# Left-over rows in places of their own, and sums of w_in formed from the operands in SBUF

## The chip, the cores and the metric

One core of one Trainium2 chip runs the kernel. The metric is device time in microseconds (us). Engines are named as in the profile: PE (matmul), PEld (its weight load), DVE (VectorE), ACT (ScalarE), POOL (GpSimd) and SP, which issues most DMAs.

## What is computed

Linear attention for 8 batches of 8 heads (576 rows, 64 columns a head), and then a gated MLP on its 4608 rows of 512 columns:

```python
q_s = softmax(q, axis=-1); k_s = softmax(k, axis=2)
kv = einsum('bhsd,bhse->bhde', k_s, v)
x  = einsum('bhsd,bhde->bhse', q_s, kv)      # heads side by side: (4608, 512)
h = x @ w_in                                  # w_in (512, 2048)
out = (h * cos(h)) @ w_out                    # w_out (2048, 512)
```

The inputs are drawn as 64-bit numbers and arrive as pairs of 32-bit words.

## The kernel before

**Tiles.** A batch gives 512 "main" rows of x and 64 left-over rows; the left-over rows of all eight batches form a ninth block of 512, collected in the HBM tensor `x_left`. A pair of heads is called p (0 to 3), a block b, a 128-wide slice of the MLP's inner dimension f (0 to 15). Each f32 operand of the MLP is held as a high and a low part, and a product takes three matmuls (hi·hi, hi·lo, lo·hi). For blocks 0 to 4 a unit (b, f) is twelve matmuls into `h` (L842), the gate on ACT and DVE (`gated`: L867, L871, L877, L882), the split into `ghi` and `glo` (L898, L902), and twelve matmuls into `acc` (L926; for the first six units eight, L919). Blocks 5 to 8 go in two pairs by `block` (L1170), with seven products in place of eight; these need sums and differences of quarters of w_in.

**Weights.** `load_w` brings a 512 KB tile of w_in (`raw_i`) or w_out (`raw_o`), and `convert` turns the 64-bit words into f32: `bias` and `bits` on ACT (L397, L402), `shift` and `sign` on DVE (L408, L419) into the place `wc`, then `hi` (L428) and `lo` (L432). For w_in, `keep` then stores the f32 rows in the HBM tensor `w_rows` (L442, SP). Later `sums(n)`, n = 0 to 7, loads two such rows back (`rows`, L997), forms sums on DVE (L1002 to L1005), splits them (L1009, L1013) and stores them in `w_sums` (L1020). `own` stores the halves of w_in themselves in `w_own` (L1023). `block` loads both through POOL (L1144).

**Attention at the start.** For block 0 and each p: column maxima of k on DVE (L536 to L545) and POOL (L551), difference and exp (L558, L564), the product kv (L602), its scaled copy `kvw` (L622); q's softmax (L649 to L668), its transpose on PE (L694, L698) and the copy `qf` (L710); then `x_mm` (L715) in two halves, the high part `x_hi` (L729), and for block 0 a second product less the high part (L715, L720) for the low part (L738). `x_hi` also copies the left-over 64 columns (L732) to `xl`, and `put` stores them (L754). For blocks below QD = 2 both `qf` and `xl` take places of the same ring `row`, which has three. From block 2 on, q is transposed through HBM into the place `qb` (L767).

**Order.** Every step is entered in a `Plan` with an engine, a duration, reads, writes and a due time; a list scheduler with these durations decides one order for all engines, and each engine then works in that order. A load has a step on SP and one on a modelled bus. The program has eight semaphores for SP's DMAs, so each issue waits until the one eight issues before has landed. An instruction that waits holds up all that stand behind it on its engine.

Of the kernel before, what the change touches and what calls it, by code (L numbers as in the profile page):

```python
# [11 lines left out]
F32 = mybir.dt.float32  # L12
# [13 lines left out]
CFG = dict(  # L26
    FH=8,
    XF=8,
    PELO=1,
    early=1,  # L30
    F2=6,
    FN=8,
    QD=2,
    warm=14,
# [8 lines left out]
    att0=dict(k=(-11.28, 5.44), kv=(18.78, -0.31), q=(5.83, 11.45), qt=(12.05, 4.95), x=(9.45, -8.71)),  # L43
    att1=(5.98, 6.97),
    std=5,
    slow=1.3,
    spans={2: (15.0, 28.0), 3: (29.0, 42.0), 4: (43.0, 56.0), 5: (52.0, 66.0), 6: (62.0, 77.0)},
    phi=0.906,
# [157 lines left out]
def linear_attention_then_cos_gated_mlp(  # L206
# [18 lines left out]
    nc = tc.nc  # L225
    B, H, S, D = q.shape
    DM = H * D
    DFF = w_in.shape[1]
    P = 128
    NP = H // 2  # L230
    CM = S // P
    NM = CM * P
    NL = S - NM
    NC = CM + 1
    KC = DM // P
    NF = DFF // P
# [12 lines left out]
    dr = ctx.enter_context(tc.tile_pool(name="dr", bufs=1, space=bass.MemoryType.DRAM))  # L249
# [38 lines left out]
    q_rows = dr.tile([2, S, P], F32, name="q_rows")  # L288
    part = dr.tile([2, NJ, P, DM], F32, name="part")
    x_main = dr.tile([B, KC, P, TB], F32, name="x_main")  # L290
    w_rows = dr.tile([NF, P, DM], F32, name="w_rows")
    w_sums = dr.tile([NF // 2, P, 4, 2, 2 * P], F32, name="w_sums")
    w_own = dr.tile([NF, P, 2, DM], F32, name="w_own")

    plan = Plan()
    plan.add("POOL", 9.0, None)
    T = {}
# [6 lines left out]
    def ring(tag):  # L304

        i = nth.get(tag, 0)
        nth[tag] = i + 1
        return (tag, i % BUFS[tag])
# [6 lines left out]
    def sbt(shape, dt, tag, name):  # L315

        pool = small if tag[0] in SMALL else sb
        return pool.tile(shape, dt, tag=tag if isinstance(tag, str) else f"{tag[0]}{tag[1]}", name=name, bufs=1)
# [63 lines left out]
    def convert(w, f):  # L382

        fs = [f] if f < FN else [base(f), base(f) + 1]
        n = len(fs)
        R = [("w", w, x) for x in fs]
        wait = w == "o" and f < F2
        C = room(f) if wait else ring("wc")

        def low():  # L390
            return T["raw", w, f][0][:, :, :, 0]

        def high():
            return T["raw", w, f][0][:, :, :, 1]

        def bias():
            nc.scalar.activation(  # L397
                high().bitcast(F32), high().bitcast(F32), AF.Identity, scale=2.0**-112
            )

        def bits():
            nc.scalar.activation(  # L402
                low().bitcast(I32), low(), AF.Identity, bias=0.4996, scale=0.875 * 2.0**-29
            )

        def shift():
            x, y = low().bitcast(I32), high().bitcast(I32)
            nc.vector.scalar_tensor_tensor(  # L408
                x, y, 3, x, op0=ALU.logical_shift_left, op1=ALU.bitwise_or
            )  # L410

        def sign():
            if wait:
                if ("room", f // 4) not in T:
                    T["room", f // 4] = sbt([P, 4, DM], F32, f"wo{room(f)[1]}", f"room_{f // 4}")
                c = T["wc", w, f] = T["room", f // 4][:, f % 4 : f % 4 + 1]
            else:
                c = T["wc", w, f] = sbt([P, 2, DM], F32, C, f"wc_{w}{f}")[:, 0:n]
            nc.vector.scalar_tensor_tensor(  # L419
                c.bitcast(I32), high().bitcast(I32), -(2**31), low().bitcast(I32),  # L420
                op0=ALU.bitwise_and, op1=ALU.bitwise_or,
            )

        def hi():
            t = T["wp", w, f] = sbt([P, n, 2, DM], F32R, spot(w, f), f"w_{w}{f}")
            for i, x in enumerate(fs):
                T["w", w, x] = t[:, i]
            nc.scalar.copy(t[:, :, 0], T["wc", w, f])  # L428

        def lo():  # L430
            t = T["wp", w, f]
            nc.vector.tensor_sub(t[:, :, 1], T["wc", w, f], t[:, :, 0].bitcast(F32))  # L432

        act, dve = (0.66, 0.69) if n == 1 else (1.1, 1.22)
        plan.add("ACT", act, bias, writes=R)
        plan.add("ACT", act, bits, writes=R)
        plan.add("DVE", dve, shift, writes=R)
        plan.add("DVE", dve, sign, reads=R, writes=[C])

        def keep():  # L440
            for i, x in enumerate(fs):
                nc.sync.dma_start(w_rows[x], T["wc", w, f][:, i])  # L442

        def split():
            plan.add("ACT", act - 0.04, hi, reads=[C], writes=R)
            plan.add("DVE", dve, lo, reads=[C], writes=R)

        if wait:
            splits[f] = split
        else:  # L450
            split()
        if w == "i":
            plan.load(0.73 * n, keep, reads=[C], writes=[("rows", x) for x in fs], parts=n)


    def load_k(b, p0, np_, tag, due, seq=()):
# [220 lines left out]
    def x_steps(b, p, place, kvw, tq, tx, due_q, due_x):  # L677
# [46 lines left out]
        def x_hi(i):  # L724
            if i == 0:
                T["x", b, p] = sbt([P, 2, TB], F32R, slot, f"x_{b}_{p}")
            cs = cols[i]
            o = T["xp", b, p, i, False]
            nc.scalar.copy(T["x", b, p][:, 0, cs], o[:, 0 : cs.stop - cs.start])  # L729
            if i == 1:  # L730
                t = T["xs", b, p] = sbt([P, NL], F32, xs, f"xl_{b}_{p}")
                nc.scalar.copy(t, o[:, TB - HALF : HALF])  # L732

        def x_lo(i):
# [40 lines left out]

        qr = [(place, 0), (place, 1)]
        cold = 2.0 if b == 0 and p < CFG["cold"] else 1.0
        qf, xs = ring("row"), ring("row")
        if blocks:
            qd, qb = ring("qd"), ring("qb")  # L780
            plan.load(1.1, q_out, reads=qr, writes=[qd], parts=2, due=due_q)
            plan.load(2.3, q_in, reads=[qd], writes=[qb], parts=4)
            plan.add("DVE", 0.75, q_blocks, reads=[qb], writes=[qf])
        else:
            if (b, p) in CFG["fill_q"]:
                fill(o1, 24, ("fill", "q", b, p), f"qt1_{b}_{p}", o1, due_q)
            plan.add(
                "PE", (0.44 if odd else 0.55) * cold, q_tr, reads=qr, writes=[o1] if odd else [o1, o2],
                due=due_q,
            )  # L790
            if not odd:
                plan.add("ACT", 0.23, q_side, reads=[o2], writes=[ring("ql")])
            plan.add("ACT", 0.82, q_f32, reads=[o1, o2], writes=[qf])
# [195 lines left out]
    def sums(n):  # L989

        f = 2 * n
# [2 lines left out]

        def rows():
            t = T["sum", n] = sbt([P, 2, DM], F32, s, f"sum_{n}")
            nc.sync.dma_start(t, w_rows[f : f + 2].rearrange("f p d -> p f d"))  # L997

        def adds():
            t = T["sum", n].rearrange("p f (k d) -> p (f k) d", k=2)  # L1000
# [21 lines left out]
        def own(x, k):  # L1022
            nc.sync.dma_start(w_own[x, :, :, k * 2 * P :], T["w", "i", x].bitcast(F32)[:, :, k * 2 * P :])  # L1023

        plan.load(0.73 * 2, rows, reads=[("rows", f), ("rows", f + 1)], writes=[s], due=due)
        plan.add("DVE", 1.8, adds, writes=[s])
        plan.add("ACT", 1.1, hi, reads=[s], writes=quarters(hs))
        plan.add("DVE", 1.22, lo, reads=quarters(hs), writes=[s])
# [2 lines left out]
        for k in range(2):  # L1031
            plan.load(
                1.46 - 0.73 * k, lambda k=k: own(f + k, k), reads=[("w", "i", f + k)], writes=[("own", f + k)],
                due=when((CFG["std"] - 2.5 + 0.18 * n) * NF),
            )

# [245 lines left out]
    def when(pos):  # L1282
        return T0 + U * pos
# [153 lines left out]
```

## Time and profile before

| | us |
|---|---|
| median of 3 runs (879.75 to 880.63) | 879.84 |
| the profiled execution's own time | 879.14 |
| its span in the trace | 877.30 |
| PE busy in the span | 855.6 |
| DVE, ACT, POOL busy | 596.9, 523.3, 77.9 |
| moved by DMA | 138.69 MB |

Times in rows are counted from the span's start. The profiled execution took 1.84 us more than its span, and the median of the runs lies 0.70 us above the profiled execution. A row of a timeline gives start, duration, engine, line, operation, output and inputs, and in brackets how long the engine had been idle and what ended that.

### The profile page before, as it was taken

The page shows a single profiled execution, that of the slowest core. Times are in us where ns is not written, and L with a number is a line of the kernel's source. Part 1 is how long each engine was busy: PE and PEld are TensorE (multiplying, and loading weights), DVE is VectorE, ACT ScalarE, POOL GpSimd, SP SyncE. Part 2 cuts the span into 40 slices and gives each one's busy share as a digit, 9 for nine tenths or more (in the row PEclk, how much of TensorE's full clock was granted, in tenths as well). Part 3 has the DMA queues.
Part 4 walks back from the last instruction along what each step waited for, and adds up shares of the span by engine and source line. Part 5 has one row for each costly group of instructions (what it writes and reads, how often), then busy time and mean ns, then how long its engine had stood idle before and what let it go on. Part 6 is the DMA issues. An engine that isn't in the chain of part 4 may idle for free.

```text
span 877.3 us, 12066 instructions
## 1 busy us (share of the span) xinstructions
PE 855.6 (98%) x4192; PEld 689.8 (79%) x4192; DVE 596.9 (68%) x961; ACT 523.3 (60%) x878; POOL 77.9 (9%) x149
## 2 busy tenths in 40 slices
PE   6889999999999999999999999999999999999998
PEld 4666688888887887888888877888888888888876
DVE  7698989996865855765885778675447937444542
ACT  3788898756555646664766646665446635444541
POOL 2100100010010010001000002111010201111000
PEclk8789999999999999999999999999999999999999
DMA  8995499924643531633797637966243726243212
GB/s 207 330 285 188 134 348 288 267 60 130 171 113 101 124 67 44 173 80 100 187 300 205 229 110 185 238 155 183 80 122 108 237 75 192 84 143 97 61 38 83
DMA packets 202556, 138.69 MB, mean 158 GB/s; under 512 B 113920, under 2 KB 174848, under 8 KB 202496
## 3 DMA queue, kind: packets, MB, share of 16 engines
q1 hardware_dynamic: 189184, 108.56, 43.9%
q0 software_dynamic: 13312, 29.36, 12.0%
q8 instruction: 33, 0.54, 0.3%
q14 instruction: 27, 0.22, 0.1%
HBM read 94.11 MB, written 43.78 MB: 157 GB/s over the span
## 4 chain that ended last, share of the span: by engine, by line
PE 93%; DMA 2%; SPq 2%; ACT 2%; DVE 1%; issue 0%; ACTq 0%
PE acc L926 42%; PE h L842 25%; PE z L1170 10%; PE a L1170 7%; PE x_False L715 4%; PE acc L919 2%; PE kv L602 2%; DMA x_left<-xl 1%; DMA raw_i<-in_moe_w_in_dram 1%; SPq L493 0%; PE qt L694 0%; SPq L489 0%; DVE kt L871 0%; PE x_True L715 0%; SPq L474 0%
## 5 line engine op out<-in xcount | busy, mean ns | idle before, releaser
L842 PE MATMUL h<-x,w_i 128*128 128x512 f32 x960 | 236.2, 397 | 0.2 <-DVE kt L882 0.2
L842 PEld LDWEIGHTS h<-x,w_i 128*128 128x128 f32 x960 | 180.8, 190 | 40.6 <-DVE kt L882 0.8
L926 PE MATMUL acc<-w_o,ghi 128*128 128x512 f32 x592 | 187.8, 398 | 0.0
L926 PEld LDWEIGHTS acc<-w_o,ghi 128*128 128x128 f32 x592 | 110.3, 188 | 24.0
L926 PE MATMUL acc<-w_o,glo 128*128 128x512 f32 x296 | 115.5, 390 | 0.0
L1170 PE MATMUL z<-xs,s 128*128 128x512 f32 x384 | 97.8, 392 | 0.5 <-DVE kt L882 0.5
L867 ACT ACTIVATE kt<-h 128x512 int32<-128x512 f32 x80 | 47.6, 597 | 67.8 <-PE h L842 66.0
L1170 PEld LDWEIGHTS z<-xs,s 128*128 128x128 f32 x384 | 71.9, 188 | 16.0 <-DVE kt L882 0.9
L871 DVE SCALAR_TENSOR_TENSOR kt<-kt,h 128x512 f32<-128x512 int32 x80 | 54.5, 682 | 40.3 <-ACT kt L867 40.1
L898 ACT CAST ghi<-kt 128x512 fp32r<-128x512 f32 x74 | 45.7, 618 | 49.9 <-PE acc L926 47.5
L1170 PE MATMUL a<-xs,s 128*128 128x512 f32 x288 | 73.9, 392 | 0.4 <-DVE kt L882 0.4
L902 DVE TENSOR_TENSOR glo<-kt,ghi 128x512 fp32r<-128x512 f32 x74 | 51.1, 690 | 31.1 <-ACT ghi L898 30.8
L926 PEld LDWEIGHTS acc<-w_o,glo 128*128 128x128 f32 x296 | 55.5, 188 | 12.0
L1170 PEld LDWEIGHTS a<-xs,s 128*128 128x128 f32 x288 | 53.9, 188 | 12.2 <-DVE kt L882 0.5
L882 DVE TENSOR_TENSOR kt<-kt,h 128x512 f32<-128x512 f32 x74 | 50.3, 681 | 17.0 <-ACT kt L877 16.3
L877 ACT ACTIVATE kt<-kt 128x512 f32<-128x512 f32 x80 | 50.4, 632 | 18.9 <-DVE kt L871 18.5
L715 PE MATMUL x_False<-qf,kvw 128*128 128x288 f32 x128 | 40.2, 430 | 2.8 <-ACT kvw L622 2.8
L1144 POOL DMA_DIRECT2D s<-w_sums x32 | 20.2, 631 | 176.0 <-PE a L1170 129.3
L1191 DVE TENSOR_TENSOR c<-a,c 128x512 f32<-128x512 f32 x32 | 22.1, 691 | 19.4 <-PE a L1170 18.3
L551 POOL PARTITION_ALL_REDUCE m<-m x32 | 26.2, 843 | 98.6 <-DVE m L545 98.4
L602 PEld LDWEIGHTS kv<-v_sb,k 128*64 128x64 f32 x600 | 21.1, 146 | 15.9 <-issue 8.6
L715 PEld LDWEIGHTS x_False<-qf,kvw 128*128 128x128 f32 x128 | 25.4, 202 | 10.4 <-ACT kvw L622 3.0
(617 smaller groups left out, 1411.5 us busy)
## 6 DMA issues: line engine op xcount, KB each, us to landing
s<-w_sums POOLq DMA_DIRECT2D x32, 512.0 KB, 4.0
q<-in_q_dram SPq DMA_DIRECT2D x32, 256.0 KB, 4.2
raw_i<-in_moe_w_in_dram SPq DMA_DIRECT2D x16, 512.0 KB, 5.7
raw_o<-in_moe_w_out_dram SPq DMA_DIRECT2D x16, 512.0 KB, 6.0
out_dram<-o SPq DMA_DIRECT2D x32, 256.0 KB, 2.8
s<-w_own POOLq DMA_DIRECT2D x16, 512.0 KB, 4.3
v_sb<-in_v_dram SPq DMA_DIRECT2D x30, 256.0 KB, 3.8
k<-in_k_dram SPq DMA_DIRECT2D x14, 512.0 KB, 4.6
```

What stands on the lines that cost most here:

```text
L551: nc.gpsimd.partition_all_reduce(T["m", b, p0][:, hs].rearrange("p h d -> p (h d)"), T["m1", b, p0][:, hs].rearrange("p h d -> p (h d)"), ...
L602: nc.tensor.matmul(x[h * D : (h + 1) * D, odd : odd + vt.shape[1]], t[:, h, c, :], vt, start=(c == CM), stop=(c == CM - 1),)
L715: nc.tensor.matmul(t[:, 0:HALF], T["kv", b, p], T["qf", b, p][:, cs], start=True, stop=not again)
L842: nc.tensor.matmul(o, a, x, start=(c == 0 and n == 0), stop=(c == KC - 1 and n == 2))
L867: nc.scalar.activation(t.bitcast(I32), src(), AF.Identity, bias=0.25, scale=1.0 / TWO_PI)
L871: nc.vector.scalar_tensor_tensor(t, t.bitcast(I32), -TWO_PI, src(), op0=ALU.mult, op1=ALU.add)
L877: nc.scalar.activation(t, t, AF.Sin, bias=0.5 * math.pi)
L882: nc.vector.tensor_mul(o, t, src())
L898: nc.scalar.copy(t, T["g", u])
L902: nc.vector.tensor_sub(t, T["g", u], T["gh", u].bitcast(F32))
L926: nc.tensor.matmul(T["acc", j], a[:, js], w, start=(first and n == 0), stop=(last and n == 2))
L1170: nc.tensor.matmul(o, a, x, start=(first and c == 0 and m == 0), stop=(c == 1 and m == 2), skip_group_check=not first,)
```

## The change

- Blocks 0 and 1: `xl` no longer takes a place of the ring `row`; the eight pieces (two blocks, four p) have places of their own in one tile that lies in `qb`, and the first load into `qb` (block 2, p = 0) waits until all eight are stored. The ring `row` then serves `qf` alone for these blocks.
- `w_rows`, its 16 stores (256 KB each) and its 8 loads (512 KB each) go. `rows` now adds the high and low parts of w_in on DVE: two additions of 128x512 for n below 4, one of 128x1024 for n from 4 on.
- `own`'s 16 stores may not stand before 205 us of the plan's own time.

```diff
+    own=205.0,
-    w_rows = dr.tile([NF, P, DM], F32, name="w_rows")
-        def keep():
-            for i, x in enumerate(fs):
-                nc.sync.dma_start(w_rows[x], T["wc", w, f][:, i])
-        if w == "i":
-            plan.load(0.73 * n, keep, reads=[C], writes=[("rows", x) for x in fs], parts=n)
...
-                t = T["xs", b, p] = sbt([P, NL], F32, xs, f"xl_{b}_{p}")
+                t = T["xs", b, p] = left_rows()
...
-        qf, xs = ring("row"), ring("row")
+        qf, xs = ring("row"), ring("row") if blocks else ("x_left", CFG["QD"] * p + b)
+        def left_rows():
+            if blocks:
+                return sbt([P, NL], F32, xs, f"xl_{b}_{p}")
+            if "x_left" not in T:
+                T["x_left"] = sbt([P, CFG["QD"] * NP, NL], F32, ("qb", 0), "x_left_rows")
+            return T["x_left"][:, xs[1]]
-            plan.load(2.3, q_in, reads=[qd], writes=[qb], parts=4)
+            old = [("x_left", i) for i in range(CFG["QD"] * NP)] if b == CFG["QD"] and p == 0 else []
+            plan.load(2.3, q_in, reads=[qd], writes=[qb, *old], parts=4)
...
-            nc.sync.dma_start(t, w_rows[f : f + 2].rearrange("f p d -> p f d"))
+            if f < FN:
+                for i in range(2):
+                    w = T["w", "i", f + i].bitcast(F32)
+                    nc.vector.tensor_add(t[:, i], w[:, 0], w[:, 1])
+            else:
+                w = T["wp", "i", f].bitcast(F32)
+                nc.vector.tensor_add(t, w[:, :, 0], w[:, :, 1])
...
-        plan.load(0.73 * 2, rows, reads=[("rows", f), ("rows", f + 1)], writes=[s], due=due)
+        plan.add(
+            "DVE", 1.38 if f < FN else 1.22, rows, reads=[("w", "i", f), ("w", "i", f + 1)],
+            writes=[s], due=due,
+        )
...
                 1.46 - 0.73 * k, lambda k=k: own(f + k, k), reads=[("w", "i", f + k)], writes=[("own", f + k)],
+                after=CFG["own"],
```

With other steps in the plan, the scheduler gives another order from the first microseconds on. Three places follow. In rows of the changed kernel the lines of attention stand six lower than in the kernel before (L558 there is L564 here) and those of the gate two higher.

Place one, ACT, first exps of block 0; `raw_i` and `raw_o` are weight tiles that have just been loaded. Before:

```order
L402 ACTIVATE raw_i_220<-raw_i_220 128x512
L564 ACTIVATE k_0_171<-k_0_171 128x640
L710 COPY qf_0_293<-qt_0_0_283 128x512
L710 COPY qf_0_293<-qt_0_0_288 128x64
L564 ACTIVATE k_1_183<-k_1_183 128x640
L704 COPY ql_0_305<-qt_0_0_288 128x64
L397 ACTIVATE raw_i_271<-raw_i_271 128x512
L656 ACTIVATE q_1_226<-q_1_226 128x1152
L622 ACTIVATE kvw_0_173<-kv_0_256,r_0_325 64x64 x2
```

The changed kernel, the same stretch, and after it the copies kvw_0 and kvw_1:

```order
L402 ACTIVATE raw_i_219<-raw_i_219 128x512
L397 ACTIVATE raw_i_249<-raw_i_249 128x512
L558 ACTIVATE k_0_170<-k_0_170 128x640
L402 ACTIVATE raw_i_249<-raw_i_249 128x512
L558 ACTIVATE k_1_176<-k_1_176 128x640
L650 ACTIVATE q_1_225<-q_1_225 128x1152
...
L616 ACTIVATE kvw_0_172<-kv_0_275,r_0_303 64x64 x2
L397 ACTIVATE raw_i_270<-raw_i_270 128x512
L704 COPY qf_1_346<-qt_0_1_331 128x512
L704 COPY qf_1_346<-ql_0_327 128x64
L397 ACTIVATE raw_o_288<-raw_o_288 128x512
L616 ACTIVATE kvw_1_174<-kv_1_306,r_1_349 64x64 x2
```

The first step of the second w_in tile now stands ahead of the exps of k_0 and k_1, and that of the first w_out tile ahead of kvw_1. On SP the second tile's load stands one place earlier, ahead of the second load of v, and the first load of k for block 1 stands behind one more w_in tile, one more w_out tile and one more load of v.

Place two, DVE, last maxima of block 0 and first of block 1 (mt_0 and mt_2 read the k of block 1 that a DMA has brought; r_3 is the reciprocal for kvw_3). Before:

```order
L536 TENSOR_TENSOR mt_0_399<-k_0_323 128x512
L558 TENSOR_TENSOR k_3_185<-k_3_185,m_3_387 128x640
L541 TENSOR_TENSOR m_1_0_432<-mt_0_399 128x256
L610 TENSOR_SCALAR r_2_436<-kv_2_401 128x1
...
L610 TENSOR_SCALAR r_3_473<-kv_3_448 128x1
...
L536 TENSOR_TENSOR mt_2_543<-k_2_483 128x512
```

The changed kernel:

```order
L530 TENSOR_TENSOR mt_0_433<-k_0_344 128x512
L552 TENSOR_TENSOR k_3_184<-k_3_184,m_3_418 128x640
L535 TENSOR_TENSOR m_1_0_449<-mt_0_433 128x256
L604 TENSOR_SCALAR r_2_455<-kv_2_407 128x1
...
L530 TENSOR_TENSOR mt_2_491<-k_2_404 128x512
L604 TENSOR_SCALAR r_3_498<-kv_3_470 128x1
```

r_3 has moved behind mt_2; mt_0 stands ahead of the subtraction for k_3 in both.

Place three, ACT and DVE, the first gates (kt_632 and kt_625 are unit 0; g is its gated value; q_0 is here the q of block 1). ACT before:

```order
L564 ACTIVATE k_2_483<-k_2_483 128x1280
L867 ACTIVATE kt_650<-h_616 128x512
L877 ACT_TABLE_LOAD
L877 ACTIVATE kt_632<-kt_632 128x512
L622 ACTIVATE kvw_1_446<-kv_1_562,r_1_586 64x64 x2
```

and in the changed kernel:

```order
L558 ACTIVATE k_2_404<-k_2_404 128x1280
L869 ACTIVATE kt_625<-h_502 128x512
L616 ACTIVATE kvw_1_507<-kv_1_559,r_1_582 64x64 x2
L397 ACTIVATE raw_o_354<-raw_o_354 128x512
L879 ACT_TABLE_LOAD
L879 ACTIVATE kt_625<-kt_625 128x512
```

DVE before:

```order
L649 TENSOR_REDUCE qm_0_669<-q_0_596 128x18
L882 TENSOR_TENSOR g_676<-kt_632,h_493 128x512
L652 TENSOR_TENSOR q_0_596<-q_0_596,qm_0_669 128x1152
```

and in the changed kernel:

```order
L643 TENSOR_REDUCE qm_0_649<-q_0_590 128x18
L604 TENSOR_SCALAR r_2_665<-kv_2_638 128x1
L607 RECIPROCAL r_2_665<-r_2_665 128x1
L646 TENSOR_TENSOR q_0_590<-q_0_590,qm_0_649 128x1152
L873 SCALAR_TENSOR_TENSOR kt_668<-kt_668,h_609 128x512
L884 TENSOR_TENSOR g_681<-kt_625,h_502 128x512
```

The copy kvw_1 of block 1 has moved ahead of the table load; the gate of unit 0 has moved behind q's subtraction and the second unit's first DVE step.

## Rows read from the trace of the kernel before

**Rows 1.** The page: busy time of PE, and in 40 slices of the span the clock granted to PE, in tenths.

```profile
PE 855.6 (98%) x4192; PEld 689.8 (79%) x4192; DVE 596.9 (68%) x961; ACT 523.3 (60%) x878; POOL 77.9 (9%) x149
...
PEclk8789999999999999999999999999999999999999
```

**Rows 2.** Busy time by stretch: the stretch and its length, then for PE, PEld, DVE, ACT, POOL busy us and instructions, granted clock (1.00 is 2.4 GHz, 0.50 is 1.2 GHz), DMA's busy share, GB/s.

```profile
14.90:20.40 5.50, 5.02 (x49) 3.99 (x49) 5.47 (x11) 1.44 (x4) 1.37 (x2) 0.50 0.83 238
35.20:38.30 3.10, 3.04 (x9) 2.46 (x10) 1.63 (x3) 2.67 (x10) 1.01 (x2) 0.52 1.04 350
38.30:48.95 10.65, 10.63 (x80) 8.07 (x79) 8.23 (x15) 10.26 (x26) 1.74 (x4) 1.00 1.06 322
...
53.00:59.00 6.00, 5.95 (x32) 4.88 (x33) 5.93 (x13) 5.36 (x8) 0.00 (x0) 0.53 0.96 316
60.00:200.00 140.00, 140.00 (x647) 106.91 (x646) 125.37 (x187) 113.44 (x185) 9.19 (x20) 1.00 0.71 212
500.00:520.00 20.00, 19.75 (x103) 15.83 (x102) 14.42 (x26) 11.03 (x19) 0.00 (x0) 1.00 0.40 129
520.00:540.00 20.00, 19.14 (x99) 14.96 (x98) 17.43 (x30) 12.84 (x25) 3.80 (x6) 1.00 0.84 214
```

**Rows 3.** Two of PE's waits from 10 to 56 us: us in total, times, the longest.

```profile
PE kv L602 <- ACT k L564: 2.3, 2, 1.2
PE qt L694 <- ACT qf L710: 2.2, 2, 1.8
```

**Rows 4.** Timeline of PE.

```profile
14.92 1.35 PE L602 MATMUL kv<-v_sb,k 128*64 128x66 f32 x20 [3.64 <-DMA v_sb<-in_v_dram]
...
23.18 2.29 PE L715 MATMUL x_False<-qf,kvw 128*128 128x288 f32 x4 [2.79 <-ACT kvw L622]
...
26.47 1.86 PE L715 MATMUL x_False<-qf,kvw 128*128 128x288 f32 x4
...
36.17 2.12 PE L715 MATMUL x_False<-qf,kvw 128*128 128x288 f32 x4
...
39.45 1.13 PE L715 MATMUL x_False<-qf,kvw 128*128 128x288 f32 x4
...
41.71 0.65 PE L715 MATMUL x_True<-qf,kvw 128*128 128x288 f32 x2
...
42.42 1.39 PE L602 MATMUL kv<-v_sb,k 128*64 128x66 f32 x40
...
50.10 0.80 PE L602 MATMUL kv<-v_sb,k 128*64 128x66 f32 x20 [1.17 <-ACT k L564]
53.05 1.35 PE L602 MATMUL kv<-v_sb,k 128*64 128x66 f32 x20 [2.15 <-ACT kvw L622]
54.34 5.00 PE L842 MATMUL h<-x,w_i 128*128 128x512 f32 x12
...
59.18 3.59 PE L919 MATMUL acc<-room,g 128*128 128x512 f32 x8
```

**Rows 5.** The chain that ended last, in order of time: start, us, what.

```profile
62.78 2.75 PE h L842 x12
...
72.94 0.97 PE x_False L715 x4
```

**Rows 6.** Timeline of ACT.

```profile
12.34 0.72 ACT L564 ACTIVATE k<-k 128x640 f32<-128x640 f32 x1
...
24.47 0.62 ACT L622 ACTIVATE kvw<-kv,r 64x64 f32<-64x64 f32 x2
...
25.54 0.67 ACT L397 ACTIVATE raw_i<-raw_i 128x512 f32<-128x512 f32 x1
...
34.63 0.70 ACT L710 COPY qf<-qt 128x512 f32<-128x512 f32 x2 [2.00 <-DMA x_left<-xl]
...
50.56 1.28 ACT L877 ACT_TABLE_LOAD   x1
...
69.43 0.70 ACT L710 COPY qf<-qt 128x512 f32<-128x512 f32 x2 [0.48 <-PE qt L694]
```

**Rows 7.** Timeline of DVE. L610 is the first of two like steps of a reciprocal r.

```profile
30.43 0.69 DVE L536 TENSOR_TENSOR mt<-k 128x512 f32<-128x512 f32 x1 [3.10 <-DMA k<-in_k_dram]
31.04 0.82 DVE L558 TENSOR_TENSOR k<-k,m 128x640 f32<-128x640 f32 x1
...
41.91 0.69 DVE L536 TENSOR_TENSOR mt<-k 128x512 f32<-128x512 f32 x1 [2.07 <-DMA k<-in_k_dram]
...
52.14 1.34 DVE L649 TENSOR_REDUCE qm<-q 128x18 f32<-128x1152 f32 x1
53.41 0.68 DVE L882 TENSOR_TENSOR g<-kt,h 128x512 f32<-128x512 f32 x1
54.00 1.35 DVE L652 TENSOR_TENSOR q<-q,qm 128x1152 f32<-128x1152 f32 x1
...
55.87 0.22 DVE L610 TENSOR_SCALAR r<-kv 128x1 f32<-128x1 f32 x1
```

**Rows 8.** Issues on SP's queue: start, us to issue.

```profile
13.65 0.62 SPq L512 DMA_DIRECT2D v_sb<-in_v_dram  x1
...
21.69 0.59 SPq L374 DMA_DIRECT2D raw_o<-in_moe_w_out_dram  x1
...
43.36 0.64 SPq L512 DMA_DIRECT2D v_sb<-in_v_dram  x1
...
45.67 1.54 SPq L493 DMA_DIRECT2D q<-in_q_dram  x1
...
47.93 1.03 SPq L493 DMA_DIRECT2D q<-in_q_dram  x1
```

**Rows 9.** DMA issues in the windows of the second w_in tile (16.28 us) and of the first w_out tile (21.69 us): KB, us from issue to landing.

```profile
raw_i<-in_moe_w_in_dram SPq DMA_DIRECT2D x1, 512.0 KB, 4.6
...
raw_o<-in_moe_w_out_dram SPq DMA_DIRECT2D x1, 512.0 KB, 6.5
```

**Rows 10.** DVE's groups by shape: count, busy us, mean ns of one, idle time before them.

```profile
L902 DVE TENSOR_TENSOR glo<-kt,ghi 128x512 fp32r<-128x512 f32 x74 | 51.1, 690 | 31.1 <-ACT ghi L898 30.8
...
L1013 DVE TENSOR_TENSOR sum<-sum,sh 128x1024 f32<-128x1024 f32 x8 | 9.7, 1220 | 1.0 <-ACT sh L1009 1.0
```

**Rows 11.** The two lines that go, on SP's queue: ns to issue (min/median/max), first and last start.

```profile
L442 SPq DMA_DIRECT2D w_rows<-wc_i x16: 319/482/1147, 28.6 to 154.5; - x16
...
L997 SPq DMA_DIRECT2D sum<-w_rows x8: 370/492/837, 162.6 to 496.5; - x8
```

## The prediction

> **What bounds the kernel now.** I read the page's first two parts, then the stretches, then the waits and timelines of the first 60 us. PE is busy 98% of the span, 855.6 us, at a granted clock that is full in nearly all slices; only the first three are lower [rows 1]. Between 500 and 540 us PE stands still for 1.1 us in all, 0.5 at the longest [rows 2]. So the number of PE's products sets the time, and the change leaves that number alone. What it can move is the start, up to about 60 us. There PE waits for the first v (3.6 us), for kvw (2.8 and 2.15), for k's exp (2.3) and for `qf` (2.2) [rows 3, 4], and these waits leave the clock at half: 14.9 to 20.4 at 0.50, 35.2 to 38.3 at 0.52, 53 to 59 at 0.53 [rows 2]. In the last, twelve products of h take 5.00 us that take 2.75 at full clock [rows 4, 5].
>
> **The change, steps with one answer.** The 16 stores and 8 loads of `w_rows` cost SP 16 x 0.48 + 8 x 0.49 = 11.6 us [rows 11] and move 8.4 of 138.69 MB. Where PE has no waits this gives nothing. `own`'s stores, the same bytes in another place, go from a start where DMA's share is 0.96 to 1.06 into a stretch where it is 0.71 [rows 2]; at nothing, hidden by PE's work there. The sums add 8 additions of 128x512 (0.69 us, the shape of L902) and 4 of 128x1024 (1.22, that of L1013), 10.4 us of DVE [rows 10]. DVE is idle 5.6 of 20 us from 500 and 2.6 of 20 from 520 [rows 2], so nearly all lies in gaps; bounds 0 and 10.4 us without any cover; I take 0.2, some of a stall like those of DVE's gate around 520.
>
> **The new order at the start**, replayed with the durations of before:
>
> 1. On ACT, L397 of the second w_in tile now stands ahead of k_0's exp. Its load takes the place of v's, issued at 13.65 [rows 8]; with the 4.6 us of the nearest such load [rows 9] it lands at 18.25, L397 ends at 18.9 and the exp, which began at 12.34 and takes 0.72 [rows 6], ends at 19.55. The first kv moves from 14.92 [rows 4] to 19.55, +4.6.
> 2. The 5.02 us of PE work from 14.9 to 20.4 [rows 2] then stand between it and the first x_False: 24.6 for 23.18 [rows 4], +1.4. The rest of the 4.6 was a wait already (2.8, for kvw).
> 3. L397 of the first w_out tile stands ahead of kvw_1. That tile was issued at 21.69 and took 6.5 us [rows 8, 9], landing at 28.2; with one load of v (288 KB, 0.9 to 1.2 us at 322 to 238 GB/s [rows 2]) fewer ahead, 27.2. L397 and kvw_1 end at 28.4 where kvw_1 ended at 25.1 [rows 6]; x_0_1 28.4 for 26.47 [rows 4], +1.9.
> 4. DVE's mt_0 waits for the k of block 1, landed at 30.43 [rows 7]. Two weight tiles and a load of v (1.31 MB) now stand ahead of it on SP, 4.0 us at 322 to 350 GB/s [rows 2]: 34.4. The subtraction for k_3 behind it ends 1.4 us later [rows 7], exp 0.7, kvw_2 0.6 [rows 6]: 37.1. So x_0_2 moves from 36.2 [rows 4] to 37.1, +0.9, though the 2.00 us that qf_2 waits for the store of `xl` [rows 6] are gone. That wait is the one that the change takes away by design; the load of k is late next.
> 5. r_3 behind mt_2: the second k lands some 2.3 us before its 41.91 [rows 7], since a store of `w_rows`, one of `xl` and an issue of 1.58 us no longer stand ahead: 39.6. r_3 ends at 40.6, kvw_3 at 41.2: x_0_3 41.2 for 39.45 [rows 4], +1.8.
> 6. From there PE worked without a gap until 48.95, 9.5 us [rows 2, 4]: now until 50.7. But the two products that waited 1.17 and 2.15 us, for the exp of k_2 and for kvw_1 [rows 4], find both ready, because kvw_1 now stands ahead of ACT's table load of 1.28 us [rows 6] and the exp is done by 48.7. They take 2 x 0.68 at full clock (0.80 with the pipeline's end), and h 2.75: 54.9, where h ended at about 59.2 [rows 4].
> 7. The first product for `acc` then waits for the gate of unit 0, which DVE now does behind q's maximum and subtraction. SP's four issues for this q stand behind a load of v that waits until the first kv of block 1 has freed its place: 43.36 before [rows 8], 44.4 now (x_0_3 +1.8, less 0.7 for the two products of x_0_3's low part, 41.71 to 42.42 [rows 4], that moved behind). Five issues at 0.64 on, v, v and three of q, comes q's last one: 47.6; before it was 47.93, with one that took 1.54 [rows 8]. From that issue to q's maximum passed 4.21 us [rows 7, 8]: 51.8. Then 1.27 (maximum), 0.35 (the two steps of r), 1.27 (subtraction), and two steps of 0.6: gate at 55.9 [rows 7]. PE stands still for 1.0 us there, a little less than the 1.17 after which the clock stayed full (kv 0.80) [rows 4]. **acc at 55.9 for 59.18, −3.3.**
> 8. ACT must keep up with the 3.3 us. From 60 to 200 us it is busy 113.44 of 140 us and DVE 125.37 [rows 2], and with equal work ACT reaches `qf` of block 1 about 1 us earlier than 69.43 [rows 6], for an x_False that began at 72.94 [rows 5]: PE may come 3.8 us earlier without meeting it. I take back 1.1 us, the sum of PE's stalls at 500 to 540 [rows 2], the only stretch with like shares where its stalls show. Bounds 0 and all 3.3.
>
> The Trainium skill (TensorE: Matmul & The Clock Gate, section "HAM oscillation — how this bites in real kernels") says that a kernel whose bursts of products are parted by waits for DMA starts each burst at the low clock. The trace agrees at 53 to 59 us (0.53). By it, the wait in step 7, put just ahead of the long row of acc, would be the wrong place for one; the rival D below gives what it would do.
>
> **Sum.** −3.3 + 1.1 + 0.2 = −2.0 on the profiled execution's 879.14: 877.1. The median lay 0.70 above that execution; so 877.8.
>
> **Rivals.**
> - **B, more gain.** Nothing is given back and transfers at 28 to 55 us run faster with 1.0 MB of `w_rows` and the early `own` stores gone: by them 35.2 to 38.3 runs at full clock, which gives 1.5 of its 3.04 us [rows 2]. Then 879.84 − 3.3 − 1.5 = 875.0. For it: share 1.04 and 1.06 there. Against: steps 3 to 5 make every x later.
> - **C, no change.** The 3.3 us are given back in 60 to 200, where DVE is busy 125.37 and ACT 113.44 of 140 us [rows 2], 90% and 81%. If ACT's `qf` or DVE's steps for block 1 end when they did, x_False begins at 72.9 as before, and PE has only moved its wait: 879 to 880. For it: ACT's wait of 0.48 before `qf` was for PE itself [rows 6], so ACT does follow; DVE leaves it only 10%. Against: PE, too, was waited for there. The Trainium skill (Perfetto Trace Analysis, section "Identifying Performance Opportunities") says that it is the most contended engine that has to be improved; taking bytes from the DMA then gives nothing. By it 879.8 would stand, and the trace agrees from 60 us on, where PE is busy 140.00 of 140.
> - **D, slower.** q lands later than in step 7. SP works in order, and ahead of q stand a store of left-over rows, two weight tiles and two loads of v; each also waits for the transfer eight issues before. With q at 53 in place of 51.8, PE would stand still for 2.2 us, as long as the 2.15 that was followed by half clock [rows 4]: from there on the case decides. With q at 54 the gate comes at 58.1; seven products of acc and what stands behind lose as much as h and kv did at 53 us, (5.00 − 2.75) + 0.55 = 2.8: 60.9 in place of 59.18, +1.7. With the give-back of 1.1 and 0.2 for the sums that is 879.84 + 3.0 = 882.8. For it: steps 1 and 4 already lean on loads that are guessed to 1 us, and 1.2 us suffice. Against: w_rows' stores no longer stand before q.
>
> **How the numbers follow.** The forecast: 0.45, with its own range 876.5 to 878.8 (give-back 0 to 2.1). B 0.13, C 0.22, D 0.20. A measurement of this kernel can tell about 0.2%, 1.76 us, from no change, that is 878.1 to 881.6. Faster: B and the forecast up to 878.1, 0.50. Same: C and the rest of the forecast, 0.30. Slower: D, 0.20. The range holds the forecast, C and most of B and D: 874.5 to 882.5; the sums without cover (10.4 us) and D's far end stay outside.
>
> **What would show it.** Right: the first kv of block 0 near 19.5; the first x_False near 24.6; no wait for `x_left` on ACT; the two kv at 50.7 without a wait and 52 to 55 at full clock; acc at 55.9 with a wait of about 1 us for DVE; x_False of block 1 near 70; PE's busy time some 2 us lower. Wrong: half clock after 52; a PE wait for ACT or DVE of over 2 us in all between 60 and 200; waits for `sum` or for DVE's gate after 440 of more than 1 us; a wait for `w_own` in the paired blocks.

## The result, and the profile after

The changed kernel takes 887.22 us (median of 5 runs, 886.67 to 888.73) beside 879.75 (median of 5 as well) for the kernel before on the same chip: ratio 1.0091, 95% interval 1.0076 to 1.0107. It is slower by 0.9%, where 877.8 was forecast with 882.5 as the upper end. The profiled execution's span is 885.9 us for 877.3: +8.6.

From the page of the changed kernel, the busy time of the engines and the clock by slice:

```profile
PE 856.2 (97%) x4192; PEld 689.2 (78%) x4192; DVE 606.3 (68%) x973; ACT 524.2 (59%) x878; POOL 77.2 (9%) x149
...
PEclk7889999999999999999999998999999999999999
```

PE does the same 4192 products in the same busy time as in [rows 1]; DVE has 9.4 us more, the additions. The loss is therefore idle time of PE in the main: 29.7 us of the span for 21.7. To find where it arises, the products of both traces were counted from the start, each weighed by its duration at full clock, and the start of the same product was compared; the difference is called the lag below. The changed kernel is behind by 1.5 us from 60 us on, 3.3 us at 490, 7.3 us at 840. Two jumps make most of it: one at the first gate, one at 520 to 540 us, where the units of block 4 give way to the paired blocks ("the passage" below).

PE's timeline of the changed kernel at the start:

```profile
19.45 1.36 PE L596 MATMUL kv<-v_sb,k 128*64 128x66 f32 x20 [8.75 <-ACT k L558]
...
23.77 1.14 PE L709 MATMUL x_False<-qf,kvw 128*128 128x288 f32 x4
...
27.21 0.72 PE L709 MATMUL x_False<-qf,kvw 128*128 128x288 f32 x2 [0.92 <-ACT x L723]
...
36.02 1.50 PE L709 MATMUL x_False<-qf,kvw 128*128 128x288 f32 x4
...
40.64 1.13 PE L709 MATMUL x_False<-qf,kvw 128*128 128x288 f32 x4
...
49.85 0.80 PE L596 MATMUL kv<-v_sb,k 128*64 128x66 f32 x20
52.24 0.80 PE L596 MATMUL kv<-v_sb,k 128*64 128x66 f32 x20 [1.59 <-DMA v_sb<-in_v_dram]
55.42 5.48 PE L844 MATMUL h<-x,w_i 128*128 128x512 f32 x12 [2.38 <-DVE g L884]
60.70 3.62 PE L921 MATMUL acc<-room,g 128*128 128x512 f32 x8
```

DVE's timeline of the changed kernel, and the granted clock of two stretches (columns as in [rows 2]):

```profile
51.23 1.35 DVE L643 TENSOR_REDUCE qm<-q 128x18 f32<-128x1152 f32 x1 [1.90 <-DMA q<-in_q_dram]
...
52.83 1.34 DVE L646 TENSOR_TENSOR q<-q,qm 128x1152 f32<-128x1152 f32 x1
...
54.69 0.68 DVE L884 TENSOR_TENSOR g<-kt,h 128x512 f32<-128x512 f32 x1
```

```profile
55.40:60.70 5.30, 5.28 (x12) 4.13 (x13) 4.28 (x9) 3.20 (x4) 0.00 (x0) 0.50 1.04 237
60.00:200.00 140.00, 140.00 (x643) 106.52 (x642) 125.58 (x186) 111.82 (x184) 8.71 (x19) 1.00 0.49 141
...
530.00:540.00 10.00, 8.96 (x41) 6.16 (x42) 8.74 (x16) 4.92 (x10) 2.52 (x4) 0.66 0.68 193
```

Up to 50 us PE stands within 1.2 us of where the forecast put it. Then the third `h` (12 products) waits for the gate of unit 0, which DVE reaches only behind q's maximum and subtraction, and it runs at half clock (0.50 granted): 5.48 us. In [rows 4, 7] this gate ended at 54.09 (53.41 + 0.68), and the third `h` started at 54.34, right behind a kv and without a wait.

The passage, PE of the changed kernel, then ACT and DVE (the cast L1091 writes a combination of x's rows for the paired blocks, `a` and `z` are these blocks' first products):

```profile
517.66 2.88 PE L844 MATMUL h<-x,w_i 128*128 128x512 f32 x12
...
523.10 2.88 PE L844 MATMUL h<-x,w_i 128*128 128x512 f32 x12
...
530.43 1.19 PE L1182 MATMUL a<-xs,s 128*128 128x512 f32 x4 [1.72 <-DVE kt L884]
532.23 1.22 PE L1182 MATMUL a<-xs,s 128*128 128x512 f32 x2 [0.61 <-DVE xs L1095]
533.43 2.93 PE L1182 MATMUL z<-xs,s 128*128 128x512 f32 x6
536.28 1.36 PE L596 MATMUL kv<-v_sb,k 128*64 128x66 f32 x20
```

```profile
526.02 0.62 ACT L1091 CAST xs<-xt 128x512 fp32r<-128x512 f32 x1 [7.16 <-PE h L844]
526.55 0.59 ACT L869 ACTIVATE kt<-h 128x512 int32<-128x512 f32 x1
```

```profile
529.69 0.68 DVE L884 TENSOR_TENSOR kt<-kt,h 128x512 f32<-128x512 f32 x1
```

The same stretch of the kernel before, PE and ACT:

```profile
517.47 5.74 PE L842 MATMUL h<-x,w_i 128*128 128x512 f32 x24 [0.25 <-DVE kt L882]
...
525.86 0.80 PE L602 MATMUL kv<-v_sb,k 128*64 128x66 f32 x20
527.05 1.94 PE L1170 MATMUL a<-xs,s 128*128 128x512 f32 x6 [0.39 <-DVE kt L882]
529.45 1.67 PE L1170 MATMUL z<-xs,s 128*128 128x512 f32 x6 [0.47 <-DVE kt L882]
```

```profile
523.24 0.62 ACT L1079 CAST xs<-xt 128x512 fp32r<-128x512 f32 x1 [2.25 <-PE h L842]
```

In both, the place of that cast is the w_in tile of f = 14 and 15, so it waits until `h` of f = 15 has read the tile; the gate of f = 14 stands behind it on ACT, and `a` needs that gate. Before, both `h` ran together, and four groups of `acc` and a kv covered the cast and the gate. After, `h` and `acc` alternate and that kv has moved behind `z`: ACT stands still for 7.16 us although `h` of f = 14 has ended near 520.5, the gate comes late, PE waits 1.72 and 0.61 us, and then runs at half clock (z 2.93).

### The profile page after: what moved, and what is told of

It reads as the page before. It is cut to its first block, busy times and chain, and to the rows that moved or that the text cites. A ratio compares the mean times of both kernels' runs of the same rounds, so it can differ in the third digit from the quotient of the medians.

```text
span 885.9 us, 12023 instructions
## 1 busy us (share of the span) xinstructions
PE 856.2 (97%) x4192; PEld 689.2 (78%) x4192; DVE 606.3 (68%) x973; ACT 524.2 (59%) x878; POOL 77.2 (9%) x149
## 4 chain that ended last, share of the span: by engine, by line
PE 92%; DMA 2%; DVE 2%; SPq 2%; ACT 1%; issue 1%; DVEq 0%; ACTq 0%
PE acc L928 42%; PE h L844 24%; PE z L1182 10%; PE a L1182 7%; PE x_False L709 3%; PE acc L921 2%; PE kv L596 2%; DMA k<-in_k_dram 1%; SPq L487 1%; DMA v_sb<-in_v_dram 0%; DMA out_dram<-o 0%; SPq L483 0%; DMA q<-in_q_dram 0%; PE x_True L709 0%; DVE kt L873 0%
## 5 line engine op out<-in xcount | busy, mean ns | idle before, releaser
L709 PE MATMUL x_False<-qf,kvw 128*128 128x288 f32 x128 | 38.2, 409 | 0.9 <-ACT x L723 0.9
L596 PE MATMUL kv<-v_sb,k 128*64 128x66 f32 (+1 forms) x600 | 25.1, 235 | 10.3 <-ACT k L558 8.8
```

What stands on the lines that cost most here:

```text
L596: nc.tensor.matmul(x[h * D : (h + 1) * D, odd : odd + vt.shape[1]], t[:, h, c, :], vt, start=(c == CM), stop=(c == CM - 1),)
L709: nc.tensor.matmul(t[:, 0:HALF], T["kv", b, p], T["qf", b, p][:, cs], start=True, stop=not again)
```

## The experiments

Each time is a median, with its ratio to the kernel before on the same chip and its 95% interval. The lag is the delay of the same product against the kernel before, in the profiled executions; the start is read at 130 us. A lag belongs to one execution, and that can lie 2 us beside the median (left_cast: 874.90 profiled, 876.96).

| run | us | ratio | lag 130 | 490 | 840 |
|---|---|---|---|---|---|
| the change | 887.22 | 1.0091 [1.0076, 1.0107] | +1.5 | +3.3 | +7.3 |
| gate_first | 882.88 | 1.0041 [1.0027, 1.0055] | −1.4 | +0.5 | +2.2 |
| cast_later | 883.78 | 1.0054 [1.0038, 1.0069] | +1.4 | +3.5 | +2.9 |
| both | 880.98 | 1.0016 [1.0006, 1.0025] | −1.6 | +0.2 | −0.5 |
| own_spread | 888.67 | 1.0100 [1.0086, 1.0114] | +3.1 | +4.9 | +6.6 |
| all_three | 881.45 | 1.0020 [1.0011, 1.0029] | +0.5 | +2.3 | +1.7 |
| new_start | 885.21 | 1.0067 [1.0053, 1.0081] | +1.7 | +3.7 | +3.9 |
| old_order | 879.62 | 1.0004 [0.9995, 1.0013] | −1.7 | +0.4 | +0.4 |
| no_adds | 877.11 | 0.9975 [0.9966, 0.9984] | −1.4 | −1.4 | −1.4 |
| sums_behind | 881.55 | 1.0017 [1.0008, 1.0025] | −2.4 | +2.4 | +2.4 |
| pool_sums | 895.39 | 1.0175 [1.0160, 1.0190] | −2.3 | +13.9 | +15.3 |
| own_late | 883.07 | 1.0045 [1.0031, 1.0059] | −2.2 | +2.8 | +2.8 |
| left_only | 879.58 | 1.0006 [0.9994, 1.0018] | −2.8 | −2.7 | +0.2 |
| left_cast | 876.96 | 0.9975 [0.9965, 0.9985] | −2.6 | −3.0 | −4.3 |
| sums_only | 885.95 | 1.0076 [1.0064, 1.0088] | +1.7 | +1.1 | +3.9 |

### The two places in the changed kernel's order

The theory: the loss is the order around two waits, not the work. **gate_first** moves one step, the gate of unit 0 on DVE, ahead of q's maximum:

```diff
+    steps = plan.order(CFG["kappa"], CFG["rounds"], CFG["tables"], CFG["alpha"]); move(steps)
+def move(steps):
+    for x, y in [(152, 151)]:
+        steps.remove(x)
+        steps.insert(steps.index(y) + 1, x)
```

> The changed kernel with one step moved: on DVE the gate of unit 0 (g from kt and h) stands ahead of q's maximum again, as it did in the kernel before. Theory A (the order at two places costs the time, and one of them is here): the gate ends at about 52.5 us instead of 55.3, the third h begins at 53 without the wait of 2.38 us and at full clock (2.75 instead of 5.48), the first product for acc begins near 56 instead of 60.7; one microsecond may come back at the fourth h. Against the changed kernel's 887.2: 883.3, between 882.0 and 884.5. Rival B (the additions on DVE and the stores that run later cost the time, whatever the order): the 3 to 5 us come back within the next 100 us, 886.5 to 887.5. Rival C (the second v, which lands at 52.2, and the load of k hold the start): acc begins at 59 or later, 886.

PE of gate_first at the start and at the passage:

```profile
52.74 0.80 PE L596 MATMUL kv<-v_sb,k 128*64 128x66 f32 x20 [1.45 <-DMA v_sb<-in_v_dram]
53.48 3.02 PE L844 MATMUL h<-x,w_i 128*128 128x512 f32 x12
56.33 3.59 PE L921 MATMUL acc<-room,g 128*128 128x512 f32 x8
61.26 3.04 PE L844 MATMUL h<-x,w_i 128*128 128x512 f32 x12 [1.33 <-DVE g L884]
```

```profile
527.59 1.20 PE L1182 MATMUL a<-xs,s 128*128 128x512 f32 x4 [1.72 <-DVE kt L884]
529.39 0.73 PE L1182 MATMUL a<-xs,s 128*128 128x512 f32 x2 [0.60 <-DVE xs L1095]
530.60 1.67 PE L1182 MATMUL z<-xs,s 128*128 128x512 f32 x6 [0.47 <-DVE kt L884]
```

`h` no longer waits and takes 3.02 us; acc starts at 56.33 for 60.70, and the time falls by 4.34 us, within theory A's range. The wait of 1.33 us behind it is new, at full clock. Not all of the 4.34 us is the start, for which the lag gives 2.9 (+1.5 to −1.4). At the passage the same 1.72 us is still there, but the clock stays full behind it, and from 490 to 840 us PE loses 1.7 us for 4.0 in the profile of the changed kernel.

**cast_later** moves the cast on ACT, the combination's low part and one difference on DVE, and one load on POOL behind the gate of f = 14:

```diff
+    for x, y in [(2010, 1645), (2011, 1646), (2023, 2011), (2050, 2023), (2051, 2050)]:
```

> The changed kernel with ACT's cast of the fifth combination of x (it takes the place of a w_in tile that the last h of block 4 still reads) moved behind the gate of the last but one unit, and what hangs on it moved with it (its low part and one difference on DVE, one load on POOL). Theory A: ACT no longer stands still for 7.2 us at 519 to 526 with that gate behind it; the first product of the paired blocks begins within 0.5 us of the last acc product, the waits of 1.7 and 0.6 us and the half clock of 530 to 538 go: 887.2 - 3.6 = 883.6, between 882.8 and 885.0. Rival B (DVE is late there because of the added sums): the product still waits for DVE for over 1.5 us, 886.5 to 887.5. Rival C: z is late next and waits as long, 886 to 887.

PE of cast_later at the passage:

```profile
528.74 1.07 PE L1182 MATMUL a<-xs,s 128*128 128x512 f32 x4
530.15 0.73 PE L1182 MATMUL a<-xs,s 128*128 128x512 f32 x2 [0.34 <-DVE xs L1095]
531.35 1.67 PE L1182 MATMUL z<-xs,s 128*128 128x512 f32 x6 [0.47 <-DVE kt L884]
```

The 1.72 us and the half clock are gone, and 3.44 us of the time, as theory A had it; waits of 0.34 and 0.47 us are left.

**both** has the two edits together.

> The changed kernel with both moves, of gate_first and of cast_later. Theory A (two separate places): the gains add, 887.2 - 4.3 - 3.4 = 879.5, between 878.7 and 880.6. Rival B (an earlier start makes the wait at 520 longer, or the reverse): 881 or more.

880.98, just above theory A's 880.6: 6.24 us come back of the 7.47 lost, less than 4.34 + 3.44 = 7.78. The lag tells why. gate_first and both start alike (−1.4 and −1.6), so the starts of the profiles are not the reason; but part of gate_first's gain is the full clock at the passage, and cast_later's gain has that part too.

### Is it the work or the order?

**old_order** does all the work of the changed kernel in the order of the kernel before, written out as a list: the additions stand where the loads stood, `own`'s stores early.

```diff
-    steps = plan.order(CFG["kappa"], CFG["rounds"], CFG["tables"], CFG["alpha"])
+    steps = STEPS
```

> All steps of the changed kernel (sums added up on DVE, no stored f32 rows, left-over rows in places of their own) in the order that the kernel before has; the additions stand where the loads of the f32 rows stood, and the stores of w_in's halves where they stood before. Theory A: the work itself costs nothing, and the wait of 2.0 us for the store of left-over rows is gone: 878.5, between 876.5 and 880.3 where the kernel before has 879.75. Rival B: the 10.4 us of additions on DVE and what they push back cost at least 2 us in any order: 882 or more.

879.62, no difference from the kernel before (−0.4 to +1.1 us). So the whole loss is order. The time lies in theory A's range, but not because the work costs nothing; the lag shows two halves that cancel: −1.7 us from the start on, where `qf` no longer waits for the store of `xl` (the kv ahead of that place starts 0.2 us earlier than before, the next kv behind it that waits 1.8), and +1.75 at 445 to 460 us. There PE and DVE of old_order read:

```profile
453.89 3.06 PE L844 MATMUL h<-x,w_i 128*128 128x512 f32 x12 [0.60 <-DVE kt L884]
457.42 3.06 PE L844 MATMUL h<-x,w_i 128*128 128x512 f32 x12 [0.48 <-DVE kt L884]
```

```profile
447.90 1.29 DVE L1002 TENSOR_TENSOR sum<-w_i 128x512 f32<-128x512 f32 x2
...
452.02 1.22 DVE L1021 TENSOR_TENSOR sum<-sum,sh 128x1024 f32<-128x1024 f32 x1
453.15 0.68 DVE L884 TENSOR_TENSOR kt<-kt,h 128x512 f32<-128x512 f32 x1
```

The additions and the sums behind them stand ahead of the gate that frees `h`.

**no_adds** is old_order without the additions; it forms the sums from the high parts of w_in alone and leaves the low parts out.

```diff
-                    nc.vector.tensor_add(t[:, i], w[:, 0], w[:, 1])
...
+                T["w", "i", f + i].bitcast(F32)[:, 0, j * 2 * P : (j + 1) * 2 * P] for i in range(2) for j in range(2)
```

> The run old_order without the additions of the high and low parts; the sums are formed from the high parts alone, so the low parts of w_in are left out of them. Theory A (the 10.4 us of added DVE work cost what PE loses at 440 to 460 us, 1.75): 877.9, between 877.0 and 878.7. Rival B (PE loses that for another reason): 879.6.

877.11, and the lag stays at −1.4 to the end: in this order DVE's additions cost 1.8 us (2.5 by the medians), all of it at that one place.

**sums_behind** (another list, the additions and sums of n = 3 behind two gates) tried to hide them.

> The run old_order, in which PE falls back by 1.75 us between 440 and 460 us where two of the eight sums (n = 2 and 3) are made; now the additions for n = 3, the sums behind them and one low part stand behind two gates on DVE instead of ahead of them. Theory A (the added 128x512 additions delay the gates for which PE waits): the waits of 0.60 and 0.48 us go, 879.6 - 1.75 = 877.9, between 877.0 and 878.7. Rival B (the gates are late there for another reason, or the delayed sums meet a later gate): 879.2 to 880.

881.55, worse, and above both ranges. The two waits went, but the sum's subtraction L1021, now at 457.14, waits for ACT and holds up q's transposition behind it: x_False waits 1.21 us and `h` 1.20, and this `h` takes 4.60 us at a granted clock of 0.63. The place moved, the price grew. **pool_sums** gives the additions to POOL in old_order.

```diff
-                    nc.vector.tensor_add(t[:, i], w[:, 0], w[:, 1])
+                    nc.gpsimd.tensor_add(t[:, i], w[:, 0], w[:, 1])
```

> The run old_order with the additions that form the f32 rows on POOL instead of DVE, at the same places of the order. Theory A (it is DVE's time that costs): 877.9, as in sums_behind. Rival B (POOL takes so much longer that the sums behind it on DVE, which wait for it, hold up the gates all the same): 879.6 or more. The length of one addition on POOL shows in the trace.

The additions of 128x512 on POOL, and the longest wait of PE:

```profile
L1002 POOL TENSOR_TENSOR sum<-w_i 128x512 f32<-128x512 f32 x8 | 11.7, 1480 | 21.8 <-DMA o<-part 7.5 <-DVE qs L654 7.2 <-issue 7.2
```

```profile
PE acc L928 <- DVE glo L904: 10.9, 2, 10.4
```

An addition takes 1480 ns there for 684 on DVE in old_order, and one wait of 10.4 us near 200 us outweighs all: 895.39.

**own_late** is old_order with `own`'s stores where the changed kernel has them (`steps = STEPS` with another list, as in own_spread, all_three, new_start and sums_behind).

> The run old_order with the 16 stores of w_in's halves where the changed kernel has them (behind the same products of PE, from about 205 us on) and not where the kernel before has them. Theory A (they hide in either place): 879.6, within 0.8. Rival B (they compete with the loads of the start): up to 1.5 less, 878.1. Rival C (in their new place they hold up SP's loads for blocks 2 to 4): 881 or more.

```profile
PE acc L928 <- DVE o L966: 1.7, 2, 0.9
```

883.07: the stores stand ahead of loads of `part` on SP, DVE's `o`, which adds what is loaded, comes late, acc waits for it (the row above, from PE's waits of own_late), x_False waits 0.6 us more, and 3 us are lost between 200 and 240. **own_spread**, on the other hand, takes the changed kernel and spreads the same stores over 205 to 430 us.

> The changed kernel with the 16 stores of w_in's halves spread out: one behind the gate of every second unit from about 205 to 430 us, instead of 14 of them between 219 and 245. All else keeps its order. Theory A (the packed stores hold up the transfers behind them on SP, and this is the 1.2 us that PE falls back between 205 and 300): 887.2 - 1.2 = 886.0, between 885.3 and 886.7. Rival B (the order of PE's small products there costs it, not the stores): 887.2, within 0.5.

The time, 888.67, lies above both ranges, since the start is 1.6 us later. Against the changed kernel the lag is flat from 130 to 490 us (+1.6 at both ends), so the crowding of the stores isn't the cause of the slow loss between 200 and 330. At the passage own_spread has the waits of the changed kernel but keeps full clock:

```profile
532.06 1.19 PE L1182 MATMUL a<-xs,s 128*128 128x512 f32 x4 [1.72 <-DVE kt L884]
...
535.06 1.66 PE L1182 MATMUL z<-xs,s 128*128 128x512 f32 x6 [0.47 <-DVE kt L884]
```

**all_three** has the two edits of both and the spread stores.

> The run both (gate of unit 0 ahead, cast behind) with the stores spread out as in own_spread. Theory A: 881.0 - 1.2 = 879.8, so that nearly all of the changed kernel's loss is accounted for by three places. Rival B: 881.0, within 0.5.

881.45, not better than both: the same answer.

**new_start** has the changed kernel's order up to the first acc, and that of the kernel before from there.

> The same work: the order of the changed kernel up to the first product for acc (60.7 us there), and from there on what is left in the order of the kernel before. Theory A: the start alone costs what it shows at that point, 1.5 us, and nothing is given back or added later: 879.75 + 1.5 = 881.3, between 880.0 and 882.5. Rival B: 885 or more. Rival D (a late start is made up, since it gives ACT and DVE a lead): 879 to 880.

885.21 was a miss. Its lag of +1.7 at 130 us is the start; another +1.7 at 450 us is old_order's price for the additions, which I had not put into the expectation.

### One part of the change alone

**left_only** is the kernel before with the left-over rows' places alone, and the planner's own order.

```diff
-        qf, xs = ring("row"), ring("row")
+        qf, xs = ring("row"), ring("row") if blocks else ("x_left", CFG["QD"] * p + b)
```

> One part alone on the kernel before: the left-over rows in places of their own; the f32 rows are stored and loaded and w_in's halves are stored early, as before. The scheduler makes its own order; the gate of unit 0 stands ahead of q's maximum in it, and at the passage to the paired blocks h and acc alternate as in the changed kernel, but with one product kv for cover. Theory A: first acc 1 to 3 us earlier than before, the passage 1 to 3 us later: 877.5 to 881.5. Rival B (the left-over rows are what made the changed kernel slow): 885 or more. Rival C (they are the gain of old_order, 1.7 us, and cost nothing): 878.

879.58, no difference, again out of two halves. The start gains 2.8 to 3.2 us; in this order the gate of unit 0 stands ahead of q. That this is about the −3.3 of the forecast is no support for it, since the forecast was made for the other order. Then the passage takes it back. PE of left_only:

```profile
522.60 0.80 PE L602 MATMUL kv<-v_sb,k 128*64 128x66 f32 x20
524.39 1.20 PE L1178 MATMUL a<-xs,s 128*128 128x512 f32 x4 [0.99 <-DVE kt L890]
526.79 0.73 PE L1178 MATMUL a<-xs,s 128*128 128x512 f32 x2 [1.21 <-DVE xs L1091]
527.99 2.53 PE L1178 MATMUL z<-xs,s 128*128 128x512 f32 x6 [0.47 <-DVE kt L890]
```

**left_cast** is left_only with the cast and what hangs on it moved, as in cast_later (eleven steps in that order's numbers, the first three shown).

```diff
+    for x, y in [(2042, 1678), (1683, 2042), (2043, 1683),
...
```

> The run left_only (left-over rows alone), in which PE is 3.2 us ahead of the kernel before at 505 us and loses 3.3 us at the passage to the paired blocks; the cast of the fifth combination stands behind the gate of the last but one unit, as in cast_later, and the last unit's gate stands ahead of the other casts. Theory A (the same mechanism as in the changed kernel): the waits of 0.99, 1.21 and 0.47 us and the half clock behind them go, 879.6 - 3.3 = 876.3, between 875.3 and 877.5, faster than the kernel before. Rival B (w's products wait for their loads next): 878 or more.

The same stretch of left_cast:

```profile
522.31 0.80 PE L602 MATMUL kv<-v_sb,k 128*64 128x66 f32 x20
523.04 1.65 PE L1178 MATMUL a<-xs,s 128*128 128x512 f32 x6
524.53 1.54 PE L1178 MATMUL z<-xs,s 128*128 128x512 f32 x6
```

No wait is left, and 876.96 beats both kernels (0.9975, 0.9965 to 0.9985).

**sums_only** is the kernel before with the sums from hi and lo alone, in the planner's own order.

```diff
-            nc.sync.dma_start(t, w_rows[f : f + 2].rearrange("f p d -> p f d"))
+                    nc.vector.tensor_add(t[:, i], w[:, 0], w[:, 1])
```

> One part alone on the kernel before: the f32 rows are neither stored nor loaded, the sums come from the high and low parts; the left-over rows take the ring, and the halves are stored early. The scheduler makes its own order; on ACT k_0's exp stands ahead of the second w_in tile's first step, as before, and the gate of unit 0 behind q's maximum alone, as before. Theory A: start like before's within 1 us, the additions cost 0 to 1.75, the passage at 520 costs -1 to +3: 879 to 884. Rival B (this is the part that makes the changed kernel slow): 886 or more.

885.95, above theory A's range: most of the change's loss comes with this one part. As far as the waits show, it is again the order that the planner gives and not the additions' time: the start loses 1.7 us, not within 1 as expected (a kv waits 4.65 us for k's exp, which stands behind the gate's table load on ACT), the passage 2.8 (z waits 3.8 us for a gate, and runs at half clock), the tail 2.7. `own`'s delay alone was not tried.

## Why the prediction was wrong, step by step

- **Steps 1 to 5, and step 6 up to its two kv, were right** to 1.2 us: the first kv at 19.45 (19.55 forecast), x_False at 23.77 (24.6), x_0_1 at 27.21 (28.4), x_0_2 at 36.02 (37.1), x_0_3 at 40.64 (41.2), the two kv at 49.85 (50.7) and both at full clock. No kv waited for kvw or k's exp there. The second waited 1.59 us for v instead, which I hadn't seen.
- **The end of step 6 and step 7 failed, though the time for the gate was right**: forecast 55.9, ends at 55.4 (54.69 + 0.68). I let the third `h` run before the gate (to 54.9) and only acc wait. But `h` has two places, and the third one needs that of unit 0, which the gate frees. So PE waited 2.38 us, 12 products ran at half clock, and acc came at 60.70: +1.5 for −3.3. No row of before shows this wait, since there the third `h` starts behind a kv, 0.25 us after the gate's end [rows 4, 7]; the two places stand in the kernel. gate_first shows it: one step moved, `h` starts without a wait, 2.9 us back at the start.
- **The largest term was missing.** I replayed the new order over the first 60 us and took the rest as it was; at the passage the order had changed as well. It costs 3.6 us in the profile (lag 3.3 at 490, 6.9 at 570); cast_later returns 3.4. About 2 of the 3.6 go with the half clock behind the waits: own_spread has the same waits, full clock and a loss of 1.5. The prediction's own signs of being wrong came here and at the start: half clock after 52 us, and a wait of over 1 us for DVE's gate after 440. The give-back of step 8 was to cover stalls at 500 to 540, sized at 1.1 us from rows of an order that no longer held.
- **Step 8**: PE doesn't meet ACT or DVE between 60 and 200 (140.00 of 140 busy), so rival C's mechanism didn't occur.
- **The sums at 0.2 us**: in the order of before they cost 1.8 (no_adds), inside the bounds 0 to 10.4. In the changed order one wait of 0.4 for a gate near 270 is all that could be theirs.
- **`own` at nothing**: wrong in the order of before (3 us, own_late), not refuted in the changed one (own_spread). The bytes were hidden; the place in SP's queue was the risk.
- **The left-over rows**: right. The wait for `xl` went, and was worth 1.7 us in an unchanged order (old_order).
- **Rival D** had the sign, the shape (a wait of over 2 us, then half clock) and, by luck, the time of acc (60.9 for 60.70), but not the cause: q wasn't late (its maximum began at 51.23, before at 52.14), and the wait stood ahead of `h` and not of acc. The other 1.3 of its +3.0 are the give-back and the sums, and it has nothing for the passage.

Together: start +1.5, 200 to 490 us +1.8, passage +3.6, 570 to 840 +0.4, tail and end +1.3, which is the +8.6. Of the 1.8 us, 0.4 is the wait near 270, 0.7 with the slower restart behind it. Most of the rest is products that took longer (the acc products of 200 to 300 average 403 ns for 397), and the traces tell where: next to the small products. Counted from the starts of products, a group of 20 kv products that stands alone between large ones costs 0.22 us beyond its own products, a group of 40 costs 0.10. Before there are 10 and 3 of them from 200 to 490 us, after 14 and 1, which makes 0.7 us. This is a count and no run tested it; the stores, at least, were ruled out. Some 0.4 us stay open, and so does the tail, where ACT waits longer for a store of `out` to free its place, in the same order. Before, then after:

```profile
851.73 0.58 ACT L967 COPY o<-acc 128x512 f32<-128x512 f32 x1 [1.21 <-DMA out_dram<-o]
```

```profile
860.28 0.58 ACT L969 COPY o<-acc 128x512 f32<-128x512 f32 x1 [2.48 <-DMA out_dram<-o]
```

old_order, no_adds, own_late, sums_behind, left_only and left_cast have 1.20 to 1.22, and gate_first, cast_later, both, all_three, own_spread, sums_only and new_start over 2. new_start (2.37) has the order of old_order from 61 us on, so the order there isn't what decides; no run told what does.

## What to carry to other kernels

When an edit makes a scheduler deal out a new order, follow the order through every change of stage, not only where the edit lies: for each instruction that stands behind a new neighbour, ask which place it waits for and which instruction frees that place. Count the places of a ring before letting a product run ahead of the gate that frees one. And cost an edit twice, in an order held fixed and in the new one; here the work was worth 0 ± 1 us and the order 7.5.

## What was not expected of the hardware

- The length of a wait doesn't by itself tell whether half clock follows. At the passage PE waited 1.72 and then 0.61 us (0.60) in the changed kernel and in gate_first, in the same sequence of products: `z` then took 2.93 us at a granted clock of 0.50 in one and 1.67 at 1.00 in the other, though the second had waited 0.47 us more before it. own_spread, which has the changed kernel's order there, had the same waits and full clock (z 1.66). The prediction took 1.17 us (full clock after it) and 2.15 (half) as two sides of a bound; these rows do not bear that out. Both of its waits, moreover, were for ACT and not for DMA [rows 4].
- The start varies between profiled executions with the same order there: the first acc of the changed kernel came at 60.70, with own_spread, the same up to 205 us, at 62.43, where the second kv of block 1 waited 2.34 us for 1.59. All four times of own_spread are high (888.33 to 889.24), so this may belong to the program rather than to the execution; it was not separated. old_order, no_adds, sums_behind and pool_sums, which differ only behind 160 us, lie 1.0 us apart at 130. By these rows a forecast of the start is good to 1 or 2 us at best.
